# Threshold instructions on ScalarE, subtractions of 1 on GpSimd, and a first attention batch in three groups: one change to a fused attention and two-layer feed-forward kernel

## The chip, the cores and the metric

The kernel runs on one NeuronCore of a Trainium2 chip. The metric is device time in microseconds (us), the median of several executions. TensorE (PE in profiles) multiplies matrices, VectorE (DVE), ScalarE (ACT) and GpSimd (POOL) do the rest, and SyncE (SP) issues most of the DMAs.

## The reference

A thresholded attention feeds two feed-forward layers. Everything is float32.

```python
batch, n_heads, seq, head_dim = (4, 8, 576, 64)
scores = matmul(q, k.transpose(0, 1, 3, 2)) / sqrt(64)
thresh = max(scores, axis=-1, keepdims=True) - tau
scores = where(scores >= thresh, scores, -1e9)
attn = exp(scores - max(scores)); attn /= sum(attn) + 1e-9
x = matmul(attn, v)                 # as [2304 tokens, 512]
h = x @ w1_in                       # 512 -> 2048
g = where(h > 0, h, exp(min(h, 0)) - 1)
x = g @ w1_out                      # 2048 -> 512
h = x @ w2_in; out = maximum(0.01 * h, h) @ w2_out
```

## The kernel before, in words

All work is recorded first as operations with dependencies (`op`, line 106), each with a due time (`vt`) and a cost for every engine that may take it. A planner (`Order.run`, line 120) then walks through model time and writes the instructions of every engine in the order in which it starts them. So the order on each engine is fixed when the program is built, and each engine works through its own list in order. The numbers that steer the planner stand in `KN` (lines 52 to 57): offsets of due times, and strings such as `kt='D'` or `km='DP'` that say which engines may take an operation (A ScalarE, D VectorE, P GpSimd).

**Attention.** A unit is 64 query rows of one pair of heads, 128 rows by 576 keys; there are 144. Units come in groups (`GROUPS`, line 31): for each batch the first 4 units and then the other 5, for 4 pairs of heads one after the other. Two units form a pair (`units`, line 464). For a unit PE makes the scores `s` (line 475). VectorE scales them into `ss` and takes the row extreme `nm` (line 479). One small instruction per pair adds tau and gives the threshold `thr` (line 485). ScalarE applies the threshold (line 490) and the exponential (line 493). VectorE inverts the sum (line 496), and GpSimd multiplies by it (line 498). Then `e` is turned, in one of two ways. Groups with a number below `GP` (line 35) are turned by PE (line 513) into PSUM and copied from there to `p` (line 510). All others are turned in 32 by 32 blocks by VectorE (line 518) and brought into place by 16 DMAs `p<-t`, 11 from SP's queue and 5 from GpSimd's (line 568). PE multiplies with `v` (line 582), and the result is copied into `x` (line 590).

**First layer, first half.** Beside the attention, blocks of 256 tokens go through the first 8 of 16 weight chunks (`block`, line 691). The first block (`NATIVE`) uses float32 matmuls (lines 621 and 674). The others split each operand into a high and a low part and need three matmuls in a reduced format (lines 624 and 678). One step takes 128 hidden columns: `h` on PE, exponential on ScalarE (line 639), minus 1 on VectorE or GpSimd (lines 641 and 643), min/max on VectorE (line 647), high part `gh` (line 652), low part `gl` (line 658), and two steps later the matmuls into `y`. When a block is done, `evac_a` (line 717) copies `y` to the staging tile `ysa` and sends it to DRAM as a partial sum `yp`.

**After the attention.** `close_attn` (line 778) gives up the attention's pools. Wide blocks of 512 tokens then run out of new tiles in the same memory: the rest of the first half, the second half of layer one, and layer two. Weights are loaded and split as they become due (`weight`, line 321; `split_w`, line 353, whose low parts `wil`, `wol` and `w` come from line 308 on GpSimd). The planner lets the pools close only when every operation recorded until then is done, and that includes the last `yp` transfer (line 799):

```python
end_a = op((HOST, 0, lambda: close_attn()), list(od.ops), [], 0)
```

Of the kernel before, what the change touches and what calls it, by code (L numbers as in the profile page):

```python
# [10 lines left out]
F32 = mybir.dt.float32  # L11
# [7 lines left out]
B, H, S, D = 4, 8, 576, 64  # L19
# [10 lines left out]
NU = S // 64  # L30
GROUPS = [(b, u0, u1) for b in range(B) for u0, u1 in ((0, 4), (4, NU))]
UM = 5
WT = 32 * UM
BESIDE = 7
GP = 1
PT = ()
NG = 5
POOLI = 520
SPI = 720
PM = ()  # L40
# [11 lines left out]
KN = dict(  # L52
    pad=18, stay=1957.74, late=1.3, margin=0, look=0.00236881, warm=2, tu=2525.65, lead=19496.6, wv0=975.379,
    wv1=-2861.01, early=3673.33, boff=26347.2, bdt=5788.03, yoff=6965.78, coff=5895.83, wb=140.292, w2a=-207.297,
    b0=0, b1=0, b2=0, bd0=9322.68, vl=22862.5, tl=13509.4, wp0=137202, wp1=-2346.6, o1=-5700.07, o2=1859.51,
    o3=-792.8, o4=-3200.93, o5=4767.88, o6=-24.0285, mo=-2162.59, ka='P', kl='PA', kh='PA', ko='P', kt='D', kx='A',
    kxl='DP', km='DP', kg='A', kgl='DP', kgl1='D', kd='P', kc='AD', kn='P', kv='AD')

# [204 lines left out]
def attn_moe_kernel(ctx, tc, kqv, tau, w1i, w1o, w2i, w2o, yp, out):  # L263
# [19 lines left out]
    wa_r = ring(stg, 1, [128, 512], F32, "wa_")  # L283
    ysx = []
    ys_r = Ring(lambda: ysx[-1], 1)
# [93 lines left out]
    rings = {True: moe_rings(sbuf(aes, "ma"), TA)}  # L379
    ysx.append(ac.tile([128, KC, TA], F32, name="ysa"))  # L380
    taut = ac.tile([128, 1], F32, name="taut")
# [45 lines left out]
    def group(gi, p, vts, held=None):  # L427
# [23 lines left out]

        by_pe = gi < GP or p in PT
        which = len(p_r.gens) % 2
# [10 lines left out]
        def units(js, vt):  # L464
# [4 lines left out]
            def qk():  # L469
                for z, j in enumerate(js):  # L470
                    for h in range(2):
                        for i in range(2):
# [11 lines left out]
                             out=thr()[:, 0:m], in0=nm()[:, 0:m], scalar1=taup, scalar2=1.0, op0=ALU.add, op1=ALU.mult)),  # L484
                         D=(150, lambda: nc.vector.tensor_scalar(  # L485
                             out=thr()[:, 0:m], in0=nm()[:, 0:m], scalar1=taup, scalar2=None, op0=ALU.add))),
# [201 lines left out]

    ypdone = {}

    def block(layer, t0, fs, tb, deps, hps, yrings, evac, vt0, dt, reg=False):
        if reg and t0 < NATIVE * TA:
            xc = [(None, x[:, k, t0:t0 + tb], deps[k]) for k in range(KC)]
        else:
            xc = conv_x(t0, tb, deps, vt0 - dt + (KN["coff"] if reg else 0), reg)
        pend, lasty = [], None
        if isinstance(yrings, Ring):
            gen = yrings.new()
            ybank = [(gen, m % 2, m % 2 == 1) for m in range(KC)]

            def ysl(yg, m):
                return yg()[:, m // 2, m % 2 * TA:(m % 2 + 1) * TA]
        else:
            ybank = [(r.new(), 0, True) for r in yrings]

            def ysl(yg, m):
                return yg()[:, 0:tb]
        for n in range(len(fs) + LAG):
            if n < len(fs):
                pend.append(step_h(layer, fs[n], tb, xc, hps, vt0 + n * dt, reg))  # L710
            if n >= LAG:
                j = n - LAG
                lasty = step_y(layer, fs[j], j == 0, j == len(fs) - 1, tb, pend[j], ybank, ysl,
                               vt0 + n * dt + (KN["yoff"] if reg else 1))
        evac(t0, tb, ybank, ysl, lasty, xc, vt0 + len(fs) * dt)

    def evac_a(t0, tb, ybank, ysl, last, xc, vt):
        ys = ys_r.new()
        done = []
        if ybank[0][0] is ybank[1][0]:  # L720
            yg = ybank[0][0]
            for j in range(2):
                done.append(op(copy_of("AD", 2 * TA, lambda j=j: ys()[:, 2 * j:2 * j + 2, 0:TA],
                                       lambda j=j: yg()[:, j, :].rearrange("p (a b) -> p a b", a=2)),
                               [last[2 * j], last[2 * j + 1]], [yg, ys], vt))
# [33 lines left out]
    for b in range(B):  # L759
        mine = [gi for gi, g in enumerate(GROUPS) if g[0] == b]  # L760
        order += [(gi, p) for p in range(NE) for gi in mine] if b in PM else [(gi, p) for gi in mine for p in range(NE)]
    kept, ready = None, {}
    for gi, p in order:
        b, u0, u1 = GROUPS[gi]
        kept, later = group(gi, p, [(u + j) * TU for j in range(u1 - u0)], kept if b in PM and u0 else None)
        u += u1 - u0
        ready[b * S + 64 * u1] = u
        if held is not None:
            held()
        held = later  # L770
        if gi < GP or p in PT or u == NP * NU:
            held()
            held = None
# [14 lines left out]

    for i in range(BESIDE):
        need = next(n for t, n in ends if t >= (i + 1) * TA)  # L790
        block(0, i * TA, list(range(FH)), TA, x_deps(i * TA, TA), h_a, ya, evac_a,
              need * TU + KN["boff"] + (KN["b0"], KN["b1"], KN["b2"], 0)[min(i, 3)], KN["bd0"] if i == 0 else KN["bdt"],
              reg=True)
        if i == NATIVE - 1:
# [3 lines left out]

    end_a = op((HOST, 0, lambda: close_attn()), list(od.ops), [], 0)
    late_pool = []  # L800
# [92 lines left out]
```

## Time and profile before

| what | us |
|---|---|
| median of 3 runs | 1043.79 (1040.55 to 1047.26) |
| the profiled execution, its own time | 1044.41 |
| the profiled execution, span of the core | 1042.6 |
| PE busy in the span | 1005.2 (96%) |
| DVE, ACT, POOL busy | 569.2, 507.0, 392.0 |

The span runs from the first to the last instruction. PE counts as busy while a matmul is in flight. The clock in the rows is the mean granted TensorE clock as a share of full speed; it has two levels, 1.2 and 2.4 GHz, so 0.5 is the lower one.

### The profile page before, as it was taken

The numbers are of one execution on the slowest core, as the hardware profiler recorded it, in microseconds if no ns is written. First come the engines' busy times: TensorE is split into PE (matmuls) and PEld (weight loads), VectorE is DVE, ScalarE is ACT, GpSimd is POOL, SyncE is SP. The second block draws the span as 40 slices with busy tenths as digits, with TensorE's granted clock in tenths as the row PEclk, the third lists the DMA queues.
The fourth block names the chain that finished last, engine by engine and source line by source line (L and its number), as shares of the span: only waits on it lengthen the run. The fifth ranks groups of instructions, "written<-read, shape, count | busy, mean of one in ns | idle before, by whom it ended". The sixth has DMA issues, their size and how long they took to land.

```text
span 1042.6 us, 17014 instructions
## 1 busy us (share of the span) xinstructions
PE 1005.2 (96%) x6228; PEld 795.3 (76%) x6228; DVE 569.2 (55%) x1146; ACT 507.0 (49%) x1009; POOL 392.0 (38%) x542
## 2 busy tenths in 40 slices
PE   6869999999999998999999999999999999999998
PEld 3446676677676776888888889888888888888898
DVE  6888778787887856767786457442211311311121
ACT  6967767677777753555455235432222311322221
POOL 5678977567577752444443013440000000000000
PEclk8999999999999999999999999999999999999999
DMA  6676876766778653353443103320100100000010
GB/s 213 209 216 175 221 195 192 227 188 196 201 209 240 192 150 119 102 182 101 143 141 101 61 21 86 118 61 0 41 1 1 41 1 1 22 19 1 1 41 21
DMA packets 47554, 115.93 MB, mean 111 GB/s; under 512 B 9776, under 2 KB 14384, under 8 KB 47472
## 3 DMA queue, kind: packets, MB, share of 16 engines
q1 hardware_dynamic: 42960, 104.36, 33.4%
q0 software_dynamic: 4512, 10.50, 3.7%
q8 instruction: 49, 0.80, 0.3%
q14 instruction: 33, 0.27, 0.1%
HBM read 67.63 MB, written 9.44 MB: 74 GB/s over the span
## 4 chain that ended last, share of the span: by engine, by line
PE 90%; DVE 3%; DMA 2%; ACT 2%; issue 1%; POOL 0%; SPq 0%; ACTq 0%; DVEq 0%; POOLq 0%
PE y L678 37%; PE h L624 22%; PE hb L624 15%; PE v L582 7%; PE s L475 7%; PE y L674 1%; DMA p<-t 1%; PE h L621 1%; DVE w L346 1%; DMA taut<-in_tau_dram 1%; DVE ss L479 1%; DMA wraw<-in_w1i_dram 1%; PE y L513 0%; DVE xl L307 0%; ACT e L493 0%
## 5 line engine op out<-in xcount | busy, mean ns | idle before, releaser
L307 DVE TENSOR_TENSOR gl<-g,gh 128x512 fp32r<-128x512 f32 (+1 forms) x150 | 101.1, 675 | 284.4 <-ACT g L656 265.0
L678 PE MATMUL y<-gh,woh 128*128 128x512 f32 (+1 forms) x704 | 245.5, 349 | 2.1 <-ACT ysa L318 1.4
L678 PE MATMUL y<-gl,woh 128*128 128x512 f32 (+1 forms) x704 | 242.8, 345 | 0.0
L624 PE MATMUL h<-xh,wih 128*128 128x256 f32 (+1 forms) x448 | 153.1, 342 | 9.2 <-ACT g L639 5.1
L678 PEld LDWEIGHTS y<-gh,woh 128*128 128x128 f32 x704 | 132.5, 188 | 29.1 <-issue 8.8
L624 PE MATMUL h<-xl,wih 128*128 128x256 f32 (+1 forms) x448 | 148.6, 332 | 0.7 <-DVE xl L307 0.6
L678 PEld LDWEIGHTS y<-gl,woh 128*128 128x128 f32 x704 | 132.7, 188 | 16.1
L498 POOL TENSOR_SCALAR e<-e,su 128x576 f32<-128x576 f32 x144 | 113.9, 801 | 32.2 <-DVE su L496 30.9
L678 PE MATMUL y<-gh,w 128*128 128x256 f32 (+1 forms) x384 | 124.9, 325 | 0.0
L490 ACT ACTIVATE ss<-ss,thr 128x576 f32<-128x576 f32 x144 | 104.6, 767 | 34.5 <-DVE thr L485 34.4
L479 DVE TENSOR_SCALAR_CACHE_REDUCE ss<-s,scl 128x576 f32<-128x576 f32 x144 | 113.8, 798 | 10.9 <-PE s L475 10.7
L678 PE MATMUL y<-gh,wol 128*128 128x512 f32 (+1 forms) x320 | 117.7, 368 | 0.0
L518 DVE STREAM_TRANSPOSE t<-e 128x640 f32<-128x640 f32 x128 | 101.2, 823 | 17.9 <-POOL e L498 12.5
L493 ACT ACTIVATE e<-ss,taun 128x577 f32<-128x577 f32 x144 | 110.5, 768 | 0.3
L624 PEld LDWEIGHTS h<-xh,wih 128*128 128x128 f32 x448 | 84.2, 188 | 33.2 <-issue 8.8
L475 PE MATMUL s<-in 64*64 64x288 f32 x1152 | 91.3, 428 | 7.8 <-DVE ss L479 7.8
L624 PE MATMUL hb<-xh,wih 128*128 128x512 f32 (+1 forms) x256 | 94.6, 369 | 0.0
L624 PE MATMUL hb<-xl,wih 128*128 128x512 f32 (+1 forms) x256 | 94.5, 369 | 0.0
L582 PE MATMUL v<-p,v 128*64 128x320 f32 (+1 forms) x640 | 87.1, 417 | 5.3 <-DVE p L319 2.3
L624 PEld LDWEIGHTS h<-xl,wih 128*128 128x128 f32 x448 | 84.3, 188 | 10.0 <-DVE xl L307 1.8
L624 PE MATMUL h<-xh,w 128*128 128x256 f32 (+1 forms) x288 | 89.3, 310 | 0.0
L654 ACT ACTIVATE gh<-h 128x512 fp32r<-128x512 f32 (+1 forms) x40 | 22.2, 555 | 132.4 <-PE h L624 132.4
(207 smaller groups left out, 1591.4 us busy)
## 6 DMA issues: line engine op xcount, KB each, us to landing
p<-t SPq DMA_DIRECT2D x128, 100.0 KB, 2.8
p<-t SPq DMA_DIRECT2D x144, 80.0 KB, 3.3
v<-in_kqv_dram SPq DMA_DIRECT2D x32, 320.0 KB, 3.8
in<-in_kqv_dram SPq DMA_DIRECT2D x16, 608.0 KB, 4.2
in<-in_kqv_dram SPq DMA_DIRECT2D x16, 544.0 KB, 4.0
wraw<-in_w1i_dram SPq DMA_DIRECT2D x16, 512.0 KB, 4.3
wraw<-in_w1o_dram SPq DMA_DIRECT2D x16, 512.0 KB, 3.6
wraw<-in_w2i_dram SPq DMA_DIRECT2D x16, 512.0 KB, 3.5
```

The costliest lines, as they stand in the source:

```text
L307: return pick(who, D=(dve(n), lambda: nc.vector.tensor_tensor(**args()), PORT), P=(pool_tt(n), lambda: nc.gpsimd.tensor_tensor(**args())))
L346: ob = op((DVE, dve(512), lambda: nc.vector.scalar_tensor_tensor(out=b().bitcast(U32), in0=top(), scalar=0x80000000, in1=b().bitcast(U32), ...
L475: nc.tensor.matmul(s[z]()[64 * h:64 * h + 64, i, 0:HALF], q()[r, at:at + 64], k()[r, h], start=True, stop=True)
L479: om = [op((DVE, dve(S) + 160, lambda z=z: nc.vector.tensor_scalar(out=ss[z]()[:, 0:S].rearrange("p (j c) -> p j c", j=2), in0=s[z]()[:, : ...
L490: o = op((ACT, act(S) + 95, lambda z=z: nc.scalar.activation(out=ss[z]()[:, 0:S], in_=ss[z]()[:, 0:S], func=AF.Prelu, bias=thr()[:, z:z + ...
L493: oe.append(op((ACT, act(S) + 190, lambda z=z: nc.scalar.activation(out=e[z]()[:, 0:S + 1], in_=ss[z]()[:, 0:S + 1], func=AF.Exp, bias=tau ...
L498: on = [op(pick(KN["kn"], P=(pool_ts(S) + 90, lambda z=z: nc.gpsimd.tensor_scalar(out=e[z]()[:, 0:S], in0=e[z]()[:, 0:S], scalar1=su()[:, ...
L518: turned.append(op((DVE, dve(SX) + 70, lambda z=z, cols=cols: nc.vector.transpose(out=blocks(tg).rearrange("p d c q -> p c d q")[:, :, :, ...
L582: nc.tensor.matmul(ps()[64 * h:64 * h + 64, 0:64 * n], v()[:, h, c, :], blocks(pg)[:, 2 * h:2 * h + 2, c], start=(c == 0), stop=(c == 4))
L624: nc.tensor.matmul(hp(), w_()[:, cs], x_()[:, 0:tb], start=(k == 0 and z == 0), stop=(k == KC - 1 and z == 2))
L654: o1 = op((ACT, actp(tb), lambda: nc.scalar.activation(out=gh()[:, cs], in_=hp(), func=AF.Prelu, alpha=0.01)), [o], [hg, gh], vt)
L678: nc.tensor.matmul(ysl(yg, m), w_()[:, cs], g_()[:, 0:tb], start=(first and z == 0 and share == 0), stop=(last and z == 2 and end))
```

## The change

Five things change, and most of the planner's numbers with them.

- `thr` may be made only by ScalarE (`kt` 'D' to 'A').
- The subtraction of 1 in a step may be made only by GpSimd (`km` 'DP' to 'P').
- Batch 0 is cut into units 0 to 3, 4 and 5, and 6 to 8, and the first two groups are turned by PE (`GP` 1 to 2).
- `ysa` moves to the pool that stays for the whole program. The pools may close before the last 256-token block's copy-out and its `yp` transfer.
- Other choices of engine: `kl` 'PA' to 'A' (low half of a raw weight), `kx` 'A' to 'PA' (high part of x), `ko` 'P' to 'PD' (low part of later weights), `kgl` 'DP' to 'P' (`gl` beside the attention).

```diff
-GROUPS = [(b, u0, u1) for b in range(B) for u0, u1 in ((0, 4), (4, NU))]
+CUTS = (4,6)
+GROUPS = [(b, u0, u1) for b in range(B) for u0, u1 in zip((0, *(CUTS if b == 0 else (4,))), (*(CUTS if b == 0 else (4,)), NU))]
-GP = 1
+GP = 2
...
-    pad=18, stay=1957.74, late=1.3, margin=0, look=0.00236881, warm=2, tu=2525.65, lead=19496.6, wv0=975.379,
+    pad=18, stay=6045.69, late=1.3, margin=0, look=0.00236881, warm=2, tu=2525.65, lead=19489.8, wv0=975.379,
...
-    ysx = []
+    ysx = [const.tile([128, KC, TA], F32, name="ysa")]
...
-    ysx.append(ac.tile([128, KC, TA], F32, name="ysa"))
...
+                         A=(200, lambda: nc.scalar.activation(
+                             out=thr()[:, 0:m], in_=nm()[:, 0:m], func=AF.Identity, bias=taup)),
-                         D=(150, lambda: nc.vector.tensor_scalar(
+                         D=(270, lambda: nc.vector.tensor_scalar(
...
     def evac_a(t0, tb, ybank, ysl, last, xc, vt):
+        since[0] = len(od.ops)
         ys = ys_r.new()
...
-    end_a = op((HOST, 0, lambda: close_attn()), list(od.ops), [], 0)
+    end_a = op((HOST, 0, lambda: close_attn()), od.ops[:since[0]], [], 0)
```

The blocks of 256 tokens (`FIRST`) are the same seven as before.

How the order moves is shown at three places. The first is ScalarE at the start of the program; `thr` is the threshold of a pair, `ss` its scores, `e` its exponentials, and `w` a raw weight's low half. Before:

```order
L338 ACTIVATE w_143<-wraw,lowb 128x512
L490 ACTIVATE ss_106<-ss_106,thr 128x576
L490 ACTIVATE ss_107<-ss_107,thr 128x576
L493 ACTIVATE e_90,su<-ss_106,taun 128x577
L493 ACTIVATE e_91,su<-ss_107,taun 128x577
```

The same place on ScalarE in the changed order:

```order
L341 ACTIVATE w_143<-wraw,lowb 128x512
L487 ACTIVATE thr<-nm,taup 128x2
L494 ACTIVATE ss_106<-ss_106,thr 128x576
L494 ACTIVATE ss_107<-ss_107,thr 128x576
L497 ACTIVATE e_90,su<-ss_106,taun 128x577
L497 ACTIVATE e_91,su<-ss_107,taun 128x577
```

Every pair has one more instruction on ScalarE, ahead of its two threshold passes, and VectorE one fewer.

The second place is PE where the second group of batch 0 begins. `s` are scores, `v` the product with the values, `y<-ident,e` a turn by PE, and `h<-x` and `y<-gh` the float32 block. Before:

```order
L621 MATMUL h<-x,w_230 128x256 x3
L475 MATMUL s<-in 64x288 x12
L621 MATMUL h<-x,w_324 128x256 x4
L674 MATMUL y<-gh,w_196 128x256 x4
L621 MATMUL h<-x,w_439 128x256 x2
L582 MATMUL v<-p_86,v 64x320 x10
L475 MATMUL s<-in 64x288 x8
```

The same place on PE in the changed order:

```order
L586 MATMUL v<-p_86,v 64x128 x10
L517 MATMUL y<-ident,e_92 128x128 x5
L625 MATMUL h<-x,w_230 128x256 x3
L517 MATMUL y<-ident,e_93 128x128 x5
L586 MATMUL v<-p_87,v 64x128 x10
L517 MATMUL y<-ident,e_90 128x128 x5
L477 MATMUL s<-in 64x288 x8
L517 MATMUL y<-ident,e_91 128x128 x5
L625 MATMUL h<-x,w_322 128x256 x2
```

Where one `v` of 320 columns stood, there are now narrow ones of 128 columns with turns between them; the `v` that depend on DMAs come after these.

The third place is VectorE where the attention ends and the 512-token blocks begin. `x<-v` is the attention's last result, `ysa` the copy-out of the last 256-token block, and `xl` the low part of the first 512-token block. Before:

```order
L647 SCALAR_TENSOR_TENSOR g<-g,h 128x256
L307 TENSOR_TENSOR gl<-g,gh 128x256
L319 COPY ysa<-y 128x512 x2
L319 COPY x<-v 128x2x5x32
L307 TENSOR_TENSOR xl_5030<-x,xh_5011 128x512
L307 TENSOR_TENSOR xl_5034<-x,xh_5028 128x512
```

The same place on VectorE in the changed order:

```order
L322 COPY x<-v 128x2x5x32
L651 SCALAR_TENSOR_TENSOR g<-g,h 128x256 x3
L322 COPY x<-v 128x2x5x32
L322 COPY ysa<-y 128x512 x2
L310 TENSOR_TENSOR xl_5146<-x,xh_5121 128x512
L310 TENSOR_TENSOR xl_5148<-x,xh_5125 128x512
```

The last `x<-v` now stands ahead of the two copies to `ysa`. On PE the last `v` stands ahead of the last 24 matmuls of the 256-token block, where it stood behind them.

## Rows read from the trace of the kernel before

**Rows 1.** Busy time by stretch: PE, PEld, DVE, ACT, POOL, clock, DMA.
```profile
0.00:56.00 56.00, 42.44 (x350) 23.25 (x352) 42.58 (x104) 45.22 (x85) 35.16 (x52) 0.91 0.66 215
56.00:80.00 24.00, 16.48 (x93) 10.32 (x91) 21.31 (x41) 15.64 (x31) 18.50 (x24) 0.87 0.66 192
...
140.00:388.00 248.00, 240.91 (x2190) 176.59 (x2187) 192.82 (x478) 181.13 (x403) 170.09 (x281) 1.00 0.70 198
388.00:406.00 18.00, 14.52 (x97) 11.77 (x98) 7.85 (x14) 4.13 (x9) 1.73 (x3) 1.00 0.52 154
406.00:572.00 166.00, 166.00 (x734) 137.46 (x733) 126.05 (x182) 88.11 (x142) 73.10 (x69) 1.00 0.40 127
```
**Rows 2.** Timeline, PE's waits from 61 to 77 us: start, length, [idle before <- releaser].
```profile
61.66 0.71 PE L475 MATMUL s<-in 64*64 64x288 f32 x8 [0.67 <-DVE ss L479]
...
64.79 0.72 PE L475 MATMUL s<-in 64*64 64x288 f32 x8 [2.41 <-DVE ss L479]
...
66.92 1.24 PE L475 MATMUL s<-in 64*64 64x288 f32 x8 [1.42 <-DVE ss L479]
...
76.56 4.93 PE L582 MATMUL v<-p,v 128*64 128x320 f32 x20 [2.20 <-DMA p<-t]
```
**Rows 3.** Chain that ended last, 0 to 100 us: start, length, what.
```profile
44.44 2.38 PE v L582 x20
...
65.34 6.51 DMA p<-t
...
92.17 2.84 PE v L582 x20
```
**Rows 4.** Timeline near 49 us: five turns by PE and the row behind.
```profile
48.58 0.77 PE L513 MATMUL y<-ident,e 128*128 128x128 f32 x5
...
49.18 0.60 PE L621 MATMUL h<-x,w 128*128 128x256 f32 x2
```
**Rows 5.** Groups by form: busy us, mean ns of one | idle before.
```profile
L490 ACT ACTIVATE ss<-ss,thr 128x576 f32<-128x576 f32 x144 | 104.6, 767 | 34.5 <-DVE thr L485 34.4
L518 DVE STREAM_TRANSPOSE t<-e 128x640 f32<-128x640 f32 x128 | 101.2, 823 | 17.9 <-POOL e L498 12.5 <-DMA p<-t 4.8 <-DMA in<-in_kqv_dram 0.2
...
L308 POOL TENSOR_TENSOR w<-w,wih 128x512 fp32r<-128x512 f32 x16 | 20.9, 1306 | 12.9 <-ACT wih L313 12.7
L308 POOL TENSOR_TENSOR gl<-g,gh 128x256 fp32r<-128x256 f32 x26 | 19.1, 734 | 14.6 <-ACT gh L313 14.2
...
L656 ACT ACTIVATE g<-hb 128x512 f32<-128x512 f32 x32 | 19.0, 593 | 0.0
L485 DVE TENSOR_SCALAR thr<-nm,taup 128x2 f32<-128x2 f32 x64 | 18.3, 286 | 0.8
...
L643 POOL TENSOR_SCALAR g<-g 128x256 f32<-128x256 f32 x41 | 17.0, 415 | 17.8 <-ACT g L639 17.5
...
L319 DVE COPY p<-y 128x640 f32<-128x640 f32 x5 | 4.1, 813 | 0.3 <-PE y L513 0.3
...
L656 ACT ACTIVATE g<-hb 128x256 f32<-128x256 f32 x8 | 3.0, 378 | 0.0
```
**Rows 6.** Waits from 0 to 90 us: total us, times, longest.
```profile
ACT ss L490 <- DVE thr L485: 7.9, 7, 2.8
```
**Rows 7.** Waits of PE from 90 to 388 us: total us, times, longest.
```profile
PE h L624 <- ACT g L639: 5.1, 10, 0.5
PE h L624 <- DVE g L647: 1.7, 3, 0.6
```
**Rows 8.** Timeline of the change to 512-token blocks.
```profile
396.50 3.12 PE L582 MATMUL v<-p,v 128*64 128x320 f32 x20
...
401.39 2.20 ACT L313 ACTIVATE xh<-x 128x512 fp32r<-128x512 f32 x4 [9.63 <-DMA yp_dram<-ysa]
...
405.74 0.40 PE L624 MATMUL hb<-xh,wih 128*128 128x512 f32 x1
```
**Rows 9.** Busy time from 95 to 140 us, columns as in rows 1.
```profile
95.00:140.00 45.00, 43.32 (x342) 29.43 (x340) 34.58 (x86) 33.18 (x73) 41.90 (x62) 1.00 0.81 222
```

More of the change, by code (lines that the diff above doesn't have):

```diff
@@ L30 @@
 NU = S // 64
-GROUPS = [(b, u0, u1) for b in range(B) for u0, u1 in ((0, 4), (4, NU))]
+CUTS = (4,6)
+GROUPS = [(b, u0, u1) for b in range(B) for u0, u1 in zip((0, *(CUTS if b == 0 else (4,))), (*(CUTS if b == 0 else (4,)), NU))]
+HEADS = [(0, 256)]
+FIRST = HEADS + [(t, TA) for t in range(256, 1792, TA)]
 UM = 5
 WT = 32 * UM
-BESIDE = 7
-GP = 1
-PT = ()
+GP = 2
+PT = set()
 NG = 5
+LP = 0
 POOLI = 520
-SPI = 720
+SPI = 700
 PM = ()
@@ L52 @@
 KN = dict(
-    pad=18, stay=1957.74, late=1.3, margin=0, look=0.00236881, warm=2, tu=2525.65, lead=19496.6, wv0=975.379,
[L54 to L57, printed above, removed]
+    pad=18, stay=6045.69, late=1.3, margin=0, look=0.00236881, warm=2, tu=2525.65, lead=19489.8, wv0=975.379,
+    wv1=-2932.64, early=5830.12, boff=34311.8, bdt=5334.25, yoff=6724.63, coff=5895.83, wb=-310.408, w2a=-3726.9,
+    b0=0, b1=0, b2=0, bd0=5160.38, vl=22862.5, tl=16711.4, wp0=137202, wp1=-414.58, o1=-5700.07, o2=-891.48,
+    o3=3737.79, o4=4188.29, o5=8465.43, o6=-22.1863, mo=-12499.3, ka='P', kl='A', kh='PA', ko='PD', kt='A', kx='PA',
+    kxl='DP', km='P', kg='A', kgl='P', kgl1='DP', kd='P', kc='AD', kn='P', kv='AD')
 PE, ACT, DVE, POOL, SP, HOST = "PE", "ACT", "DVE", "POOL", "SP", "HOST"
@@ L450, in q @@
             return kq()[:, at0:at0 + 128 * n]
-        by_pe = gi < GP or p in PT
+        by_pe = gi < GP or (gi, p) in PT
         which = len(p_r.gens) % 2
@@ L689, in attn_moe_kernel, with block @@
     ypdone = {}
-    def block(layer, t0, fs, tb, deps, hps, yrings, evac, vt0, dt, reg=False):
-        if reg and t0 < NATIVE * TA:
+    since = [0]
+    def block(layer, t0, fs, tb, deps, hps, yrings, evac, vt0, dt, reg=False, whole=False):
+        if whole:
             xc = [(None, x[:, k, t0:t0 + tb], deps[k]) for k in range(KC)]
@@ L701, in ysl @@
             def ysl(yg, m):
-                return yg()[:, m // 2, m % 2 * TA:(m % 2 + 1) * TA]
+                return yg()[:, m // 2, m % 2 * TA:m % 2 * TA + tb]
         else:
@@ L722, in evac_a @@
             for j in range(2):
-                done.append(op(copy_of("AD", 2 * TA, lambda j=j: ys()[:, 2 * j:2 * j + 2, 0:TA],
-                                       lambda j=j: yg()[:, j, :].rearrange("p (a b) -> p a b", a=2)),
+                done.append(op(copy_of("AD", 2 * tb, lambda j=j: ys()[:, 2 * j:2 * j + 2, 0:tb],
+                                       lambda j=j: yg()[:, j, :].rearrange("p (a b) -> p a b", a=2)[:, :, 0:tb]),
                                [last[2 * j], last[2 * j + 1]], [yg, ys], vt))
@@ L762, in attn_moe_kernel @@
     kept, ready = None, {}
+    PT.update(order[len(order) - LP:])
     for gi, p in order:
@@ L770, in attn_moe_kernel @@
         held = later
-        if gi < GP or p in PT or u == NP * NU:
+        if gi < GP or (gi, p) in PT or u == NP * NU:
             held()
@@ L787, in x_deps @@
                  if b * S + 64 * u0 < t0 + tb and b * S + 64 * u1 > t0] for k in range(KC)]
[L789 to L793, printed above, removed]
+    for i, (t0, tb) in enumerate(FIRST):
+        need = next(n for t, n in ends if t >= t0 + tb)
+        block(0, t0, list(range(FH)), tb, x_deps(t0, tb), h_a, ya, evac_a,
+              need * TU + KN["boff"] + (KN["b0"], KN["b1"], KN["b2"], 0)[min(i, 3)],
+              KN["bd0"] if i < NATIVE else KN["bdt"], reg=True, whole=i < NATIVE)
         if i == NATIVE - 1:
@@ L814, in dt @@
         return 24 * mm(tb)
-    rest = [(t0, tb) for t0, tb in ((t, min(TB, NT - t)) for t in range(BESIDE * TA, NT, TB))]
+    rest = [(t0, tb) for t0, tb in ((t, min(TB, NT - t)) for t in range(sum(FIRST[-1]), NT, TB))]
     ysb = {}
```

## The prediction

> **What bounds the kernel now.** I read the busy time by stretch first [rows 1]. From 406 us to 572 us PE is busy for 166.00 of 166.00 us at full clock, and it stays so to the last few microseconds. Nothing that the other engines gain there can shorten the run. The change can pay only before 406 us. There PE idles 13.6 of the first 56 us (56.00 - 42.44), 7.5 us from 56 to 80, 7.1 us from 140 to 388, and 3.5 us from 388 to 406. The clock column adds a little: 0.87 from 56 to 80 us, a mix of the 1.2 and 2.4 GHz levels, costs at most 0.13 x 24 = 3.1 us against full clock. So about 32 us of idle time and some 8 us of low clock (5 of them in the first 56 us) are all there is to win, 3 to 4% of the run, and part of the first 56 us is loading.
>
> Then I read what PE waits for, in the timeline and the waits. From 61 to 77 us it waits three times for VectorE's pass over the scores, 0.67 + 2.41 + 1.42 = 4.5 us, and once for the DMAs `p<-t`, 2.20 us [rows 2]. The chain that ended last runs through those DMAs too: a piece of 6.51 us starts at 65.34 [rows 3]. Between 90 and 388 us PE's named waits are for the exponential (5.1 us in 10 places) and for the min/max (1.7 us in 3 places) of the step before [rows 7]. They are short stalls between two steps.
>
> **The second group of batch 0, turned by PE.** The v that waited 2.20 us is replaced by narrow ones that need no DMA, and the v that still need one have a stretch of the float32 block ahead of them. I count the 2.20 us as gone. Of the 4.5 us for VectorE, its own load decides: by the order it has, between the units 17 and 24, 4 transposes fewer (4 x 0.823), 5 thresholds fewer (5 x 0.286) and 3 copies from PSUM more (3 x 0.813) [rows 5], so 3.3 + 1.4 - 2.4 = 2.3 us less. I take 2.3 us off the waits. If PE idles less there, it keeps its clock: the v at 76.56 us took 4.93 us, against 2.84 us at full clock [rows 2, 3]. I take the whole 3.1 us of rows 1 as gone. That makes 2.2 + 2.3 + 3.1 = 7.6 us.
>
> Against it, PE has more to do. Eight units are turned by PE: 8 fives of matmuls, 0.60 us from the start of a five to the next row [rows 4], 4.8 us. Four v of 320 columns (2.84 us each) become four of 128 and four of 192. From 256 to 320 columns a v grows from 2.38 to 2.84 us [rows 3], 0.46 us per 64 columns, so 1.46 + 1.92 - 2.84 = 0.54 us more each time, 2.2 us. Together 7.0 us. The idle time that I leave in this stretch, 7.5 - 2.2 - 2.3 = 3.0 us, lies between scores and turns, and I let it take up as much of them. 4.0 us remain. Net: -3.6 us. Bounds: -7.6 if all of the new work hides, and +7.0 if it all counts and no wait goes.
>
> **Thresholds on ScalarE.** VectorE gives up 80 instructions; 64 of them took 286 ns [rows 5]. No row shows this one on ScalarE. Its pass over 576 columns with a threshold as bias takes 767 ns, and 512 columns against 256 cost 593 - 378 = 215 ns more, 0.84 ns a column [rows 5]. For 2 columns that leaves 767 - 574 x 0.84 = 285 ns. The nearest bounds are 0 (all in idle time) and 767 ns. ScalarE is busy 45.22 of the first 56 us, most of the rest being its start [rows 1], so I look at batch 0: 36 units are 20 instructions, 20 x 0.285 = 5.7 us more work. But ScalarE waited 7.9 us for thresholds up to 90 us [rows 6], because they stood in VectorE's queue behind longer work. Now it waits only for the pass over the scores. I let the two cancel: 0, with +5.7 and -7.9 us as ends. After batch 0 ScalarE is busy 181 of 248 us [rows 1], and the instruction hides.
>
> The Trainium skill speaks against this edit: "ScalarE: Activation LUTs", section "Rules for kernel authors", gives additions to VectorE, and its section on ACT_TABLE_LOAD states 280 ns + 0.833 ns per column for an activation whose bias is a pointer. For 2 columns that is an estimate of 282 ns, and the row's 285 ns agrees. By the rule the edit loses what ScalarE gains in work; that is the second rival below.
>
> **Subtractions of 1 on GpSimd, and steps beside the attention.** On GpSimd one takes 415 ns at 256 columns [rows 5], still one link of the same chain. What counts is where the planner puts the next step. I counted in the order. A step whose first matmuls follow the step before with no other PE work, while ScalarE still reads that one: 9 places before, 5 now. At 5.1 / 10 = 0.51 us each [rows 7] this gives -2.0 us. A step that waits for the min/max with less than 2.3 us of PE work in between: 3 places before, 14 now. The three had 1.4 to 1.5 us in between and waited 1.7 / 3 = 0.57 us, so the link takes about 2.0 us. With 1.2 to 2.2 us in between, the 14 come to some 4.4 us, 2.7 us more than before. Net +0.7 us. Bounds: -6.8, if all waits of rows 7 go, and +7, if the link grows by half a microsecond at 14 places.
>
> **ysa outlives the attention.** The last v starts at 396.50 and ends at 399.62 us; ScalarE's first xh waits for the yp DMA and starts at 401.39; the second step's first matmul starts at 405.74 [rows 8]. That is 6.1 us from the last old work on PE to the second step. In the changed order the xh no longer waits for yp, but the new tiles still lie on tiles that the last y matmuls read, so they wait for these. From xh to the second step took 4.35 us; with 0.1 us to start, 4.45 us. Gain: 6.1 - 4.45 = 1.7 us. Bounds: 0, if the copies to ysa on VectorE push the xl back, and 3.5 us, all the idle time of the stretch [rows 1]. What comes next is again the xh and xl of the wide block.
>
> **After 406 us** PE is full and the other engines have room (VectorE 126 of 166 us, GpSimd 73 [rows 1]). Moving subtractions to GpSimd and low parts to VectorE costs nothing as long as that cover holds. Without it, one late weight is a wait of some microseconds; I allow 0 to +4.
>
> **Sum**, against the profiled execution's own 1044.41 us: -3.6 + 0 + 0.7 - 1.7 = -4.6, so 1039.8 us. The median of the runs is 0.6 us below that execution, so the forecast is 1039.2 us.
>
> **Rivals.**
> 1. VectorE's relief reaches further. It loses thresholds and subtractions all through the attention, and the waits behind it shrink everywhere. For it: the longest waits of PE name VectorE [rows 2]. Against it: between 140 and 388 us only 7.1 us are idle. Three quarters of 7.5 + 7.1 + 3.5 us idle and 3.1 us clock are 15.9 us; less 7.0 us of work, and half of the 7.9 us in rows 6, this is -12.9: about 1031 us.
> 2. ScalarE is the early bound, as the rule above has it. All 5.7 us count, and none of its waits comes back: 1039.2 + 5.7 = 1044.9 us, no change. For it: 45.22 us of the first 56.
> 3. GpSimd becomes the bound while the units 37 to 72 run, about 95 to 185 us. By the order it has 5 low parts (1306 ns), 6 subtractions (415 ns) and 2 gl (734 ns) more there [rows 5]: 6.5 + 2.5 + 1.5 = 10.5 us. From 95 to 140 us it is already busy 41.90 of 45.00 us [rows 9]. If it falls behind, every normalisation and DMA issue is late, and PE with it. It decides from the point where GpSimd has no idle time left. If all 10.5 us show, and the clock falls as it did at 61 to 77 us (3.1 us), 1039.2 + 13.6 = 1052.8 us. Against it: the planner may fill the later half, and VectorE is lighter.
>
> The Trainium skill, "SBUF — State Buffer", section "Who interferes with whom", would make rival 3 worse: a GpSimd instruction and a VectorE one with two inputs exclude each other for the whole instruction. No row here separates that.
>
> **How the numbers follow.** The sum is the likeliest case, chance 0.47, with 1035 to 1044 us as its own range. Rival 1 has 0.27, rival 2 has 0.12, rival 3 has 0.14. One per cent, about what a measurement of this kernel tells from no change, is 1033.4 and 1054.2 us. Faster by more than that: most of rival 1 and a little of the sum's edge, 0.31. Slower: part of rival 3 and of a late weight after 406 us, 0.11. The same: 0.58. The range goes down to 1028 us, rival 1 with some more, and up to 1053 us, rival 3.
>
> **What would show it.** Right: the first v of the second group starts without a DMA in front, the clock from 56 to 80 us is near 1.00, PE's waits for the min/max rise and those for the exponential fall, and from the last y of the 256-token blocks to the second wide step pass about 4.5 us. PE stays at 166 of 166 us afterwards. Wrong: PE idles in the first 56 us by more than now with ScalarE full (rival 2), GpSimd without idle time from 95 to 140 us (rival 3), or gaps on PE after 406 us.

## The result, and the profile after

| | us |
|---|---|
| kernel before, median of 4 runs beside it | 1043.09 (1040.55 to 1047.26) |
| changed kernel, median of 4 runs | 1058.68 (1055.66 to 1060.54) |
| ratio | 1.0144, 95% interval 1.0108 to 1.0181 |
| the profiled execution of the changed kernel, own time and span | 1057.34, 1055.5 |

The change makes the kernel 1.4% slower. The forecast was 1039.2 us, and its range ended at 1053. Of the runs below, one execution of E5 took 2579 us, and E5's median is that of its other three.

The busy time of the changed kernel by stretch answers to [rows 1] (PE, PEld, DVE, ACT, POOL, clock, DMA):

```profile
0.00:56.00 56.00, 42.65 (x321) 22.92 (x321) 38.69 (x87) 43.19 (x87) 27.93 (x47) 0.82 0.62 206
56.00:80.00 24.00, 22.03 (x226) 15.05 (x225) 21.66 (x45) 22.89 (x51) 15.24 (x22) 1.00 0.73 224
80.00:140.00 60.00, 55.73 (x432) 38.40 (x431) 42.49 (x95) 42.77 (x99) 52.35 (x79) 0.97 0.69 194
140.00:388.00 248.00, 233.98 (x2118) 169.71 (x2117) 173.16 (x395) 189.84 (x440) 188.85 (x312) 1.00 0.71 196
388.00:406.00 18.00, 17.25 (x137) 15.01 (x136) 6.63 (x15) 6.72 (x18) 9.56 (x17) 1.00 0.59 159
406.00:572.00 166.00, 163.68 (x741) 134.18 (x740) 121.42 (x172) 80.79 (x133) 57.31 (x72) 1.00 0.39 125
418.00:1037.00 619.00, 619.00 (x2946) 521.79 (x2945) 257.22 (x385) 204.50 (x365) 97.36 (x125) 1.00 0.18 57
```

The kernel before had one row here that [rows 1] leaves out:

```profile
80.00:140.00 60.00, 58.32 (x452) 38.34 (x449) 46.55 (x117) 44.19 (x96) 53.99 (x79) 1.00 0.76 206
```

The stretch minus PE's busy time is its idle time. From 56 to 80 us it fell from 7.5 to 2.0 us, and the clock rose to 1.00: that is where the second group stands, and the gain is there. But from 80 to 140 us idle time rose from 1.7 to 4.3 us, and from 140 to 388 us from 7.1 to 14.0 us. The clock of the first 56 us fell from 0.91 to 0.82. From 418 us on PE is full. So everything was lost before: the second wide step began at 418.87 us instead of 405.74 [rows 8], 13.1 us later, and the whole span is 12.9 us longer. PE's timeline of the changed kernel, the last old matmul and the first of the second wide step:

```profile
413.64 0.28 PE L682 MATMUL y<-gh,w 128*128 128x256 f32 x1
...
418.87 0.39 PE L628 MATMUL hb<-xh,wih 128*128 128x512 f32 x1
```

The span's 12.9 us split in two. PE's busy time rose from 1005.2 to 1014.8 us, 9.6 us: the mean clock of 0.992 before and 0.989 after costs (0.011 x 1055.5) - (0.008 x 1042.6) = 3.3 us of it by estimate, and the 6.3 us that remain are put down to added matmuls. Idle time rose from 37.4 to 40.7 us, 3.3 us. The prediction had +7.0 us of matmuls, -3.1 us of clock and -8.5 us of idle time. The matmuls came as forecast; the clock and the idle time did not.

PE's waits over the whole span (total us, times, longest) answer to [rows 2, 7]:

```profile
PE h L628 <- DVE g L651: 8.2, 14, 0.9
PE y L517 <- ACT p L321: 5.6, 5, 2.0
PE v L586 <- DMA p<-t: 4.9, 3, 2.3
PE s L477 <- DVE ss L481: 3.4, 2, 2.8
...
PE h L628 <- ACT g L643: 2.4, 5, 0.5
```

The first and the last row have the counts of the prediction: 14 waits for the min/max, 5 for the exponential. The 14 cost 8.2 us, not 4.4. The third row is a wait that the prediction had counted as gone: one of 2.2 us before, three of together 4.9 us now. PE's timeline has the first of them behind the second group:

```profile
90.38 1.13 PE L625 MATMUL h<-x,w 128*128 128x256 f32 x4
93.50 3.92 PE L586 MATMUL v<-p,v 128*64 128x192 f32 x20 [1.99 <-DMA p<-t]
```

The chain that ended last in the stretch from 85 to 98 us shows what it hangs on (start, length, what): SP's queue issues the turning DMAs one behind the other, 0.59 us each, until 90.2 us, and the last transfer takes 3.03 us more.

```profile
89.64 0.59 SPq L572
90.23 0.04 issue
90.28 3.03 DMA p<-t
```

The waits for the min/max aren't what is left of a chain from `h` through the exponential and the subtraction, as the prediction had them. The timeline of PE and VectorE at one of the 14:

```profile
209.82 0.28 PE L628 MATMUL h<-xh,w 128*128 128x256 f32 x1
210.21 0.42 DVE L651 SCALAR_TENSOR_TENSOR g<-g,h 128x256 f32<-128x256 f32 x1 [0.40 <-PE h L628]
210.68 0.38 PE L628 MATMUL h<-xh,wih 128*128 128x256 f32 x1 [0.58 <-DVE g L651]
```

VectorE waits here for PE, then PE for VectorE. In 12 of the 14 places, and in all three of the kernel before, the min/max starts 0.04 to 0.11 us after PE has ended an `h` matmul of a later step, takes 0.42 us, and PE goes on 0.05 us later (0.15 once). The wait is 0.51 to 0.66 us each time, whatever PE did between. Both steps' `h` are halves of one tile (`hbank`), and the planner has put the min/max between two matmuls into it; that the common tile is why they wait for each other is a reading of the order, which no run takes apart.

### The profile page after: what moved, and what is told of

It reads as the page before. It is cut to its first block, busy times and chain, and to the rows that moved or that the text cites. A ratio compares the mean times of both kernels' runs of the same rounds, so it can differ in the third digit from the quotient of the medians.

```text
span 1055.5 us, 17444 instructions
## 1 busy us (share of the span) xinstructions
PE 1014.8 (96%) x6348; PEld 803.8 (76%) x6348; DVE 548.2 (52%) x1030; ACT 514.5 (49%) x1067; POOL 394.3 (37%) x604
## 4 chain that ended last, share of the span: by engine, by line
PE 88%; POOL 3%; ACT 3%; DMA 2%; DVE 2%; issue 2%; SPq 1%; DVEq 0%; ACTq 0%; POOLq 0%
PE y L682 35%; PE h L628 21%; PE hb L628 15%; PE v L586 7%; PE s L477 6%; PE y L517 1%; DMA p<-t 1%; PE y L678 1%; PE h L625 1%; POOL e L502 1%; SPq L572 1%; DVE g L651 1%; ACT e L497 1%; DMA taut<-in_tau_dram 1%; ACT ss L494 1%
## 5 line engine op out<-in xcount | busy, mean ns | idle before, releaser
L310 DVE TENSOR_TENSOR gl<-g,gh 128x512 fp32r<-128x512 f32 (+1 forms) x121 | 81.2, 671 | 266.9 <-ACT g L660 257.7
L502 POOL TENSOR_SCALAR e<-e,su 128x576 f32<-128x576 f32 x144 | 109.4, 767 | 20.6 <-DVE su L500 18.0
L314 POOL TENSOR_SCALAR xh<-x 128x512 fp32r<-128x512 f32 (+1 forms) x19 | 12.8, 677 | 268.2 <-PE hb L628 259.7
L522 DVE STREAM_TRANSPOSE t<-e 128x640 f32<-128x640 f32 x120 | 96.7, 830 | 20.5 <-POOL e L502 14.6
L647 POOL TENSOR_SCALAR g<-g 128x256 f32<-128x256 f32 (+1 forms) x104 | 52.9, 509 | 138.7 <-ACT g L643 137.6
L586 PE MATMUL v<-p,v 128*64 128x256 f32 (+3 forms) x720 | 89.2, 391 | 5.9 <-DMA p<-t 4.9
```

Source lines behind the costliest of these rows:

```text
L310: return pick(who, D=(dve(n), lambda: nc.vector.tensor_tensor(**args()), PORT), P=(pool_tt(n), lambda: nc.gpsimd.tensor_tensor(**args())))
L314: return pick(who, P=(pool_ts(n), lambda: nc.gpsimd.tensor_scalar(out=dst(), in0=src(), scalar1=1.0, scalar2=1.0, op0=ALU.mult, op1=ALU.mu ...
L502: on = [op(pick(KN["kn"], P=(pool_ts(S) + 90, lambda z=z: nc.gpsimd.tensor_scalar(out=e[z]()[:, 0:S], in0=e[z]()[:, 0:S], scalar1=su()[:, ...
L522: turned.append(op((DVE, dve(SX) + 70, lambda z=z, cols=cols: nc.vector.transpose(out=blocks(tg).rearrange("p d c q -> p c d q")[:, :, :, ...
L586: nc.tensor.matmul(ps()[64 * h:64 * h + 64, 0:64 * n], v()[:, h, c, :], blocks(pg)[:, 2 * h:2 * h + 2, c], start=(c == 0), stop=(c == 4))
L647: P=(pool_ts(tb), lambda: nc.gpsimd.tensor_scalar(out=g()[:, cs], in0=g()[:, cs], scalar1=-1.0, scalar2=1.0, op0=ALU.add, op1=ALU.mult))),
```

## The experiments

The planner arranges the whole order anew whenever one of its inputs changes. So there are two kinds of experiment here. In E1 to E4, E13 and E16 PE's order of matmuls is kept, and only an engine or the end of the attention is changed; in the others the order is arranged anew. (E13 and E16 differ from their kernels in a few matmuls behind 485 us.) "Us" is the median; the ratio is to the kernel before on the same chip.

**E1 and E2: the changed kernel's order, one kind of instruction back on VectorE.** The planner still thinks the work is on GpSimd (E1) or ScalarE (E2), so the instruction stands at the same place.

```diff
-P=(pool_ts(tb), lambda: nc.gpsimd.tensor_scalar(out=g()[:, cs], in0=g()[:, cs], scalar1=-1.0, scalar2=1.0, ...
+P=(pool_ts(tb), lambda: nc.vector.tensor_scalar(out=g()[:, cs], in0=g()[:, cs], scalar1=-1.0, scalar2=None, ...
...
-A=(200, lambda: nc.scalar.activation(out=thr()[:, 0:m], in_=nm()[:, 0:m], func=AF.Identity, bias=taup)),
+A=(200, lambda: nc.vector.tensor_scalar(out=thr()[:, 0:m], in0=nm()[:, 0:m], scalar1=taup, scalar2=None, op0=ALU.add)),
```

E1: 

> The order of the changed kernel is kept word for word; only the 104 subtractions of 1 that it gives to GpSimd are issued on VectorE at the same places. Theory L (the link): the steady stretch from 140 to 388 us lost some 8 us because a subtraction on GpSimd makes the link from h to the min/max longer at 14 places. Then PE's waits for the min/max fall from 8.2 us to 2 to 4 us, the second wide step comes 5 to 8 us earlier, and the kernel takes about 1051 us. Theory O (the order): the planner's order with its new numbers and groups carries the loss, whichever engine subtracts. Then the time stays within 2 us of 1058.7.

E2: 

> The order of the changed kernel is kept; only the 80 thresholds are issued on VectorE, at the places in the order where ScalarE had them. Theory A (ScalarE is the early bound): the 20 thresholds of batch 0 cost ScalarE some 6 us, so the start up to the units of batch 1 is 3 to 6 us shorter and the kernel takes 1053 to 1056 us. Theory O: the thresholds hide, and the time stays within 2 us of 1058.7; or it gets longer by up to 8 us, if the threshold now waits behind longer work on VectorE as it did before.

Measured: E1 1060.93 us, ratio 1.0157 (1.0114 to 1.0199); E2 1060.64 us, 1.0162 (1.0121 to 1.0202). Neither brings anything back. In E1 PE's waits for the min/max stay (from 80 to 388 us; the changed kernel had 7.7 us in 13 places there):

```profile
PE h L628 <- DVE g L651: 7.9, 15, 0.9
```

The subtraction itself is no longer on GpSimd. These are the groups by form of line 647 (busy us, mean ns of one), first of the changed kernel:

```profile
L647 POOL TENSOR_SCALAR g<-g 128x512 f32<-128x512 f32 x40 | 26.7, 668 | 107.8 <-ACT g L643 107.8
L647 POOL TENSOR_SCALAR g<-g 128x256 f32<-128x256 f32 x64 | 26.2, 409 | 30.9 <-ACT g L643 29.8 <-DVE w L349 0.6
```

and here of E1:

```profile
L647 DVE TENSOR_SCALAR g<-g 128x256 f32<-128x256 f32 x64 | 33.2, 519 | 21.3 <-ACT g L643 20.6
...
L647 DVE TENSOR_SCALAR g<-g 128x512 f32<-128x512 f32 x40 | 18.1, 452 | 26.4 <-ACT g L643 26.3
```

All 104 together take 52.9 us on GpSimd and 51.3 on VectorE. Theory L falls, because the waits stay with the subtraction on VectorE: the link is not what makes them. Theory A finds no gain for E2.

**E3 and E4: the kernel before in its own order, one kind moved.** The same two swaps the other way: 60 subtractions to GpSimd, 80 thresholds to ScalarE.

E3: 

> The order of the kernel before is kept; only the 60 subtractions of 1 on VectorE are issued on GpSimd at the same places, so that all 104 are there, with the old groups and the old numbers. Theory L: PE's waits between 140 and 388 us grow by 5 to 8 us and the kernel takes 1048 to 1051 us. Theory O: within 2 us of 1043.1.

E4: 

> The order of the kernel before is kept; only the 80 thresholds are issued on ScalarE at the same places. Theory A: ScalarE's added work of batch 0 shows, the units of batch 0 end 3 to 6 us later and the kernel takes 1046 to 1049 us. Theory O: within 2 us of 1043.1. If the end of the waits behind VectorE decides, it is 2 to 5 us faster.

Measured: E3 1044.42 us, 1.0007 (0.9988 to 1.0026), no change. E4 1046.31 us, 1.0024 (1.0005 to 1.0042), 2.5 us slower. E4 lies in the range of theory A (1046 to 1049), but not by its mechanism: PE's matmul that stands at 80 us in the kernel before comes 0.3 us earlier in E4's trace, so batch 0 does not end later. A threshold on ScalarE took 286 ns there, the 285 that the prediction had worked out. So under the old order these two engine choices cost some 3 us of the 15 together, at most 7 by their intervals. The other choices (`kl`, `kx`, `ko`, `kgl`, and `kgl1` from 'D' to 'DP', which the list of the change leaves out) were never swapped alone under a kept order.

**E5 and E15: the new groups alone; E6: all but the new groups.**

```diff
-GROUPS = [(b, u0, u1) for b in range(B) for u0, u1 in ((0, 4), (4, NU))]
+CUTS = (4,6)
+GROUPS = [(b, u0, u1) for b in range(B) for u0, u1 in zip((0, *(CUTS if b == 0 else (4,))), (*(CUTS if b == 0 else (4,)), NU))]
-GP = 1
+GP = 2
```

E5: 

> The kernel before with batch 0 in three groups and its first two groups turned by PE, old numbers and old engine choices. Theory G (groups): the 6.5 us of added PE work come to no idle time, so this edit alone costs 4 to 8 us: 1047 to 1051 us. Theory N (numbers): the planner's new numbers carry the loss, and this edit is worth the -3.6 us that the prediction gave it: 1039 to 1041 us. The planner arranges the whole order anew, so some 2 us either way are put down to that.

E6: 

> The changed kernel with the old groups and only group 0 turned by PE; new numbers, new engine choices, ysa as in the changed kernel. Theory G: PE's work up to the second wide step falls by 6.5 us and the time by 4 to 8 us, to 1051 to 1055 us. Theory N: the new numbers keep the steady stretch 8 us longer, and the lost gain in the units 4 to 8 comes back as waits: 1058 to 1064 us.

Measured: E5 1061.91 us, 1.0175 (1.0158 to 1.0192); E6 1068.53 us, 1.0240 (1.0215 to 1.0264). Both are slower than either theory had it, and they contradict each other if an edit has a price of its own: added to the kernel before, the groups make it 18 us slower, and taken out of the changed kernel they make that 10 us slower, too. E15 is E5 once more, for a trace:

E15: 

> The new groups alone, once more, for a trace of an undisturbed execution: about 1062 us. It took 14 us more than the changed kernel with old numbers, which has these groups too. If thresholds and subtractions on VectorE are what the new groups do not bear, PE's waits for VectorE (s behind ss, h behind g) between 0 and 140 us hold most of the 14 us. If it is the order, the loss is spread over waits of other kinds or lies in the steady stretch from 140 to 388 us.

Measured: 1062.98 us, 1.0188 (1.0159 to 1.0217). E15 by stretch:

```profile
56.00:80.00 24.00, 23.84 (x234) 16.63 (x233) 20.07 (x43) 21.70 (x46) 15.42 (x23) 1.00 0.65 208
80.00:140.00 60.00, 49.65 (x335) 31.41 (x333) 41.76 (x95) 32.22 (x68) 47.72 (x69) 0.89 0.58 163
140.00:388.00 248.00, 236.86 (x2143) 172.57 (x2141) 193.52 (x473) 178.10 (x395) 170.16 (x279) 1.00 0.68 195
```

From 56 to 80 us PE is busy for 23.84 of 24 us: the groups do there what the prediction said. From 80 to 140 us it loses 10.4 us and the clock falls to 0.89. No engine is full there. Its waits in that stretch name the min/max of the float32 block (3.9 us), the exponential (2.5), scores (1.4) and others. VectorE's load is not it: VectorE is busy for 41.76 us there, 46.55 in the kernel before, and the waits for VectorE up to 140 us come to 13.6 us against 11.7. That leaves the order, which this run does not vary by itself.

**E7 and E8: the planner's numbers.** E7 is the changed kernel with all numbers of `KN` as before (the strings for the engines stay new); E8 is the kernel before with the new numbers alone. In both the order is arranged anew.

```diff
-    pad=18, stay=6045.69, late=1.3, ...
+    pad=18, stay=1957.74, late=1.3, ...
```

E7: 

> The changed kernel with the old numbers of the planner (not the strings that say which engines may take an operation). Theory N: the steady stretch from 140 to 388 us loses its extra 8 us and the kernel takes about 1050 us or less. Theory G: within 2 us of 1058.7.

E8: 

> The kernel before with the new numbers of the planner alone: old groups, old engine choices, old ysa. Theory N: the steady stretch is 6 to 10 us longer, 1049 to 1054 us. Theory G: within 3 us of 1043.1.

Measured: E7 1048.20 us, 1.0047 (1.0028 to 1.0067); E8 1064.18 us, 1.0194 (1.0177 to 1.0211). E7 is as theory N had it: with the same groups, engines and ysa, 10.5 us came back. E8 is 10 us above N's range. (`SPI`, the planner's 720 ns for each of SP's turning DMAs, became 700 outside `KN`; neither the list of the change nor any run here has it alone.) E7 by stretch, then its waits of PE from 80 to 388 us:

```profile
0.00:56.00 56.00, 42.55 (x326) 22.28 (x326) 40.15 (x89) 44.62 (x88) 31.84 (x50) 0.88 0.62 211
56.00:80.00 24.00, 22.72 (x214) 16.08 (x215) 17.25 (x40) 22.13 (x48) 13.37 (x20) 1.00 0.63 210
80.00:140.00 60.00, 55.90 (x468) 39.76 (x468) 42.64 (x98) 44.97 (x106) 57.43 (x85) 1.00 0.67 189
140.00:388.00 248.00, 242.24 (x2178) 178.47 (x2175) 175.94 (x401) 190.02 (x444) 193.69 (x323) 1.00 0.71 201
```
```profile
PE h L623 <- ACT g L638: 3.8, 9, 0.7
PE h L623 <- DVE g L646: 2.3, 4, 0.6
...
PE v L581 <- DMA p<-t: 0.8, 1, 0.8
```

Idle time from 140 to 388 us is 5.8 us, below the kernel before (7.1), with all subtractions on GpSimd and GpSimd busier than ever (193.69 us). The waits for the min/max fall from 13 places to 4, and those for the DMAs `p<-t` from 4.9 to 0.8 us. So neither the groups nor the engine choices by themselves lose the steady stretch: under the old numbers, with both, it is whole.

**E9 to E12: which of the numbers.** The changed kernel with one set of numbers back: `stay`; the dues of the 256-token blocks; the offsets of the stages; the dues of loads and weights.

```diff
-stay=6045.69
+stay=1957.74
...
-boff=34311.8, bdt=5334.25, yoff=6724.63, bd0=5160.38
+boff=26347.2, bdt=5788.03, yoff=6965.78, bd0=9322.68
...
-o2=-891.48, o3=3737.79, o4=4188.29, o5=8465.43, o6=-22.1863, mo=-12499.3
+o2=1859.51, o3=-792.8, o4=-3200.93, o5=4767.88, o6=-24.0285, mo=-2162.59
...
-lead=19489.8, wv1=-2932.64, early=5830.12, wb=-310.408, w2a=-3726.9, tl=16711.4, wp1=-414.58
+lead=19496.6, wv1=-2861.01, early=3673.33, wb=140.292, w2a=-207.297, tl=13509.4, wp1=-2346.6
```

E9: 

> The changed kernel with one number of the planner set back: stay from 6045.69 to 1957.74 ns, the margin by which PE keeps to the format it is in. Theory S (format runs): a larger margin makes PE stay with steps while scores and turns wait and the other way round, so that steps follow each other while their elementwise chain is still under way; then this number alone brings back most of the 10.5 us that all old numbers brought back: 1048 to 1053 us, with more changes of format on PE. Theory D (dues of the blocks), theory F (dues of the attention's stages and of the elementwise work): within 3 us of 1058.7.

E10: 

> The changed kernel with the old due times of the 256-token blocks (boff, bdt, bd0, yoff). In the changed kernel these blocks are due 8 us later against the units and their steps 0.45 us closer to each other. Theory D: the later dues leave PE without steps early and crowd them later; setting them back gives 1048 to 1053 us. Theories S and F: within 3 us of 1058.7.

E11: 

> The changed kernel with the old offsets of the attention's stages (o2 to o6) and of the elementwise work of a step (mo). Theory F: with mo at -12.5 us and the exponentials at -0.9 us the other engines serve steps ahead of units, or units ahead of steps, in a way that leaves PE waiting; setting them back gives 1048 to 1053 us. Theories S and D: within 3 us of 1058.7.

E12: 

> The changed kernel with the old due times of loads and weights (wv1, early, wb, w2a, wp1, tl, lead). Theories S, D and F: within 3 us of 1058.7. If it is faster by 5 us or more, the low halves of the weights on ScalarE at the start, or the loads after the attention, carried the loss.

Measured: E9 1054.42 us, 1.0095 (1.0080 to 1.0110); E10 1054.68, 1.0087 (1.0052 to 1.0121); E11 1052.70, 1.0072 (1.0057 to 1.0087); E12 1058.51, 1.0132 (1.0116 to 1.0149). Against 1058.68 that is -4.3, -4.0, -6.0 and -0.2 us; by the ratios, which allow for the chip, -5.1, -5.9, -7.5 and -1.3 us of the 10.1 that all of them brought back in E7. No single set carries it all, and together they would bring back twice as much. E11 just reaches the range that theory F gave it, but by F the runs E9 and E10 should have stayed within 3 us of 1058.7, and neither did; S and D miss their own ranges, too. So none of the three, each of which wanted one culprit, holds.

**E13 and E16: ysa alone, from both sides.** E13 gives the kernel before the change's lines on ysa; E16 takes the last of them out of the changed kernel.

```diff
-    end_a = op((HOST, 0, lambda: close_attn()), list(od.ops), [], 0)
+    end_a = op((HOST, 0, lambda: close_attn()), od.ops[:since[0]], [], 0)
```

E13: 

> The kernel before with ysa in the pool that stays and the pools closing without the last block's copy-out and transfer; nothing else. By the prediction's step on ysa, 1.7 us less: 1041 to 1043 us, with the stretch from the end of the last v to the second wide step 4.5 us instead of 6.1. If the wait only moves to the y matmuls' tiles, no change within 1 us.

E16: 

> The changed kernel with the pools closing only after the last block's copy-out and its transfer. Up to 405 us the order is the same. If the step on ysa was right in size, 1.5 to 3.5 us longer: 1060 to 1062 us. If ysa is worth nothing, within 1 us of 1058.7.

Measured: E13 1041.11 us, 0.9977 (0.9958 to 0.9996). PE's timeline at the transition:

```profile
395.63 1.97 PE L581 MATMUL v<-p,v 128*64 128x320 f32 x12
398.32 0.50 PE L623 MATMUL h<-xh,wih 128*128 128x512 f32 x1 [0.72 <-ACT xh L313]
...
401.79 0.39 PE L623 MATMUL hb<-xh,wih 128*128 128x512 f32 x1
```

The last v ends at 397.60, the second wide step starts at 401.79: 4.2 us, where the prediction said 4.45 and the kernel before took 6.1 [rows 8]. E13 beats both kernels.

E16: 1065.29 us, 1.0204 (1.0169 to 1.0240), 6.6 us above the changed kernel. PE's timeline of E16 at the second wide step and the next:

```profile
425.14 0.39 PE L628 MATMUL hb<-xh,wih 128*128 128x512 f32 x1
...
431.35 0.79 PE L628 MATMUL h<-xh,wih 128*128 128x512 f32 x1 [3.34 <-DVE g L651]
```

Not all that the profiled execution lost is ysa's: in the same order of PE it is 6.3 us behind the changed kernel at the second wide step (425.14 against 418.87), and the gap before that step is much the same (5.2 against 5.0 us). Behind it comes a wait of 3.34 us that the changed kernel doesn't have, with a clock of 0.86 from 425 to 437 us, and at the end the span is 11.1 us longer. So in this pair of executions, one of each, some 5 us go with the missing line, and not where the prediction looked.

**E14: the engine choices and ysa, without groups and numbers.**

```diff
-CUTS = (4,6)
-GP = 2
+GP = 1
...
-    pad=18, stay=6045.69, late=1.3, ...
+    pad=18, stay=1957.74, late=1.3, ...
```

> The changed kernel with the old groups and the old numbers: what is left of the change is the choice of engines and ysa. If the new groups cost 4.7 us by themselves (the changed kernel with old numbers took 1048.2 us, that is 4.7 us more than before), this is 1041 to 1044 us. If the engine choices cost it and the groups are free, 1047 to 1050 us.

Measured: 1052.53 us, 1.0087 (1.0058 to 1.0117), outside both ranges expected. That is 4.3 us slower than E7, which has the new groups on top. The groups that were a loss in E5 are a gain here.

**E17 and E18: an edit without a meaning.** The planner reckons 1 ns more per instruction.

```diff
-    pad=18,
+    pad=19,
```

E17: 

> The kernel before, with one number that has no meaning for the work: the planner reckons 19 ns instead of 18 ns on top of every instruction of the other engines. Instructions, groups and engine choices stay possible as before, but the order is arranged anew. Theory T (the order as a whole decides, and the numbers of the kernel before happen to fit it): several us slower, 1047 to 1060 us. Theory E (the edits themselves decide: groups, engine choices, the size of stay or of the dues): within 2 us of the kernel before.

E18: 

> The changed kernel with the same meaningless number, 19 instead of 18 ns. Theory T: the time moves by several us in either direction, 1050 to 1066 us. Theory E: within 2 us of 1058.7.

Measured: E17 1055.87 us, 1.0112 (1.0059 to 1.0165); E18 1058.78 us, 1.0146 (1.0110 to 1.0182). A number that changes nothing of the work costs the kernel before 12 us, as theory T had it, and the changed kernel nothing, which theory E had expected. E17 by stretch:

```profile
0.00:56.00 56.00, 42.55 (x309) 22.59 (x309) 39.30 (x91) 40.06 (x76) 28.12 (x46) 0.79 0.56 189
...
80.00:140.00 60.00, 51.97 (x375) 32.84 (x373) 48.01 (x106) 37.91 (x81) 52.85 (x72) 0.94 0.71 194
140.00:388.00 248.00, 238.72 (x2165) 173.42 (x2167) 193.65 (x473) 181.64 (x402) 172.20 (x283) 1.00 0.68 195
```

The pattern is that of the changed kernel: a lower clock at the start, idle time from 80 to 140 us (8.0 us) and more of it in the steady stretch (9.3 us). Here it comes from a new arrangement alone.

**What follows from all of them.** Arranged anew are the changed kernel, the groups alone (E5 and E15), E6 to E12, E14, E17 and E18: twelve arrangements. They take 1048.2 to 1068.5 us, half of them below and half above 1057 us. The changed kernel lies in the middle. All are slower than the kernel before. The same edit has another price, even another sign, by what it is combined with:

| groups | engines and ysa | numbers | us |
|---|---|---|---|
| old | old | old (before) | 1043.1 |
| new | old | old (E15) | 1063.0 |
| old | new | old (E14) | 1052.5 |
| new | new | old (E7) | 1048.2 |
| old | old | new (E8) | 1064.2 |
| old | new | new (E6) | 1068.5 |
| new | new | new (the changed kernel) | 1058.7 |

So the runs bear out this: the arrangement before was better than any of the twelve, and the change gives it up for an ordinary one. That a new arrangement alone can cost as much is shown, by one nudge of one kernel (E17). Which share of the 15 us each number has is not settled, and E9 to E12 speak against there being one. New groups with old engines under the new numbers weren't tried. (Rows with new engines have `SPI` at 700, the others at 720.)

## Why the prediction was wrong, point by point

- **Second group turned by PE (-3.6).** Right: the waits from 61 to 77 us and the low clock there are gone, and the added matmuls came to 6.3 us (7.0 forecast). Wrong: "I count the 2.20 us as gone". The reason given, a float32 block ahead of the v that still need DMAs, did not hold at 93.50 us, where 1.99 us of idle time came back, and the clock from 80 to 140 us fell to 0.97 (0.03 x 60 = 1.8 us). Local sum: 5.5 us idle time and 3.1 us clock gained, 6.3 + 2.0 + 1.8 us lost: +1.5 instead of -3.6.
- **Thresholds on ScalarE (0, between -7.9 and +5.7).** The duration was right (estimated 285 ns, measured 286 and 287). The cost in the old order is +2.5 us (E4). The rule of the Trainium skill ("ScalarE: Activation LUTs", "Rules for kernel authors"), that additions belong on VectorE, has the right sign there, by 2.5 us. In the new order going back to VectorE gains nothing (E2). It isn't the cause.
- **Steps beside the attention (+0.7, up to +7).** The counts were right, 5 and 14. The size was off: the 14 places cost 0.59 us each, 8.2 us in all, instead of 4.4. With the exponential's 2.4 us that makes 10.6 us where 6.8 us stood before: +3.8. The mechanism was wrong: the prediction took a link of about 2.0 us and let PE's work in between count against it, but the wait is a hand-over from PE to VectorE and back, 0.57 us in the rows of the kernel before too [rows 7], and 14 x 0.57 = 8.0 us would have been the price. E1 and E3 show that the engine of the subtraction doesn't matter to it. The rest of the 9.5 us of idle time added from 80 to 388 us are 4.9 us behind the DMAs `p<-t`, where there were none, and 1.3 us for the min/max of the float32 block.
- **ysa (-1.7).** Right, and shown by E13: -2.4 us (0.4 to 4.4). In the changed kernel the gap is 5.0 us (413.92 to 418.87); E16 has 5.2 us there without ysa, and its loss comes behind.
- **After 406 us (0).** Right, once the wide blocks have begun: 619.00 of 619.00 us.
- **Rivals.** None was it. VectorE's relief (rival 1) happened, 569.2 to 548.2 us busy, and bought nothing. ScalarE (rival 2) was busy for 43.19 of the first 56 us, less than before. GpSimd (rival 3) was less busy from 95 to 140 us than before, 37.91 against 41.90, and more from 95 to 185 us, 79.29 against 73.92. It came near its limit from 140 to 170 us, 28.85 of 30 us, and there PE was busy for 29.43 us, as before (29.47). In E7 GpSimd was busiest of all while PE hardly waited.
- **The step that failed** is the sum itself: the prediction priced the places that the edits name and took the rest of the order to be as good as before. Not in the sum are the first 56 us, where the clock fell by 0.09 (at most 5.0 us), and most of the 9.5 us of idle time from 80 to 388 us, of which 4.9 us are waits for DMAs `p<-t`, the kind that it had counted as gone. The count of the order covered only the places that the edits touch. A rival "a new arrangement is some 10 us worse than this one" was missing; all twelve arrangements are worse, by 5 to 25 us. Why this arrangement of the changed kernel is as slow as it is, edit by edit, stays open.

## What to carry to other kernels

Where a planner writes the order of the whole program, an edit has no price of its own: first nudge numbers that mean nothing, more than one, and see how far the time moves (here 12 us and 0), and take that as the least uncertainty of any forecast. Price an engine choice by swapping the engine under the kept order. A gain that acts behind the arranged part, as ysa does, was had alone (E13): it is the one to keep.

## What the runs showed of the hardware that had not been expected

- VectorE's time depends on GpSimd for some instructions and not for others. In the trace of E1 a subtraction of 128x256 takes a median of 289 ns on VectorE where GpSimd computes nothing beside it (32 places) and 673 ns where GpSimd is at work when it starts (29 places). In the kernel before it is 228 against 365 ns for a threshold of 128x2, and 692 against 1136 ns for a low part `gl` of 128x512. The min/max of 128x256, which reads `h` from PSUM, took 420 ns either way, and the turn of 128x640 took 833. The prediction found no row that separates the two engines; these do, and the min/max, which has two inputs as well, isn't slowed. GpSimd's own median for the subtraction of 128x256 is 403 ns in the changed kernel, so VectorE is the faster one alone and the slower one beside GpSimd. Moving 60 of them changed the whole by 0.7 us (-1.3 to 2.7).
- The clock of the first 56 us goes with PE's order: 0.82 in the changed kernel and in E1, E2 and E16, which share its order; 0.91, 0.91, 0.91 and 0.88 in the kernel before, E3, E13 and E4, which share the other. From 30 to 40 us it is 0.66 in all of the first four, and 0.83 to 1.00 in the others.
- With PE's order kept, single executions of the changed kernel, E1, E2 and E16 still lie between 1055.7 and 1068.4 us.
